# Weight words shifted in PSUM, 128-row tiles of v, and another order of the first chunk

## The chip, the cores and the metric

The kernel runs on one core of one Trainium2 chip. The metric is the device time of one execution in microseconds (us); lower is better. A core has TensorE (PE; its weight loads are PEld), VectorE (DVE), ScalarE (ACT), GpSimd (POOL) and SyncE (SP), each with its own queue that is worked off in order, and 16 DMA engines. SBUF is the working memory. PSUM is where TensorE writes; it has 8 banks of 512 fp32 words for each of 128 partitions, and GpSimd does not work on it.

## The reference

Attention in which each query sees the keys fewer than 16 positions away and 24 block summaries (the maximum of each block's 32 keys, the mean of its 32 values), and behind it two dense layers with an ELU between them. Batch 4, 8 heads, 768 positions, head size 64; the dense layers are 512 to 2048 to 512.

```python
k_sum = k.reshape(B, H, nb, block, D).max(axis=3)
v_sum = v.reshape(B, H, nb, block, D).mean(axis=3)
scores_l = scale * np.matmul(q, k.transpose(0, 1, 3, 2))
mask_l = np.abs(pos[:, None] - pos[None, :]) < window
scores_s = scale * np.einsum('bhsd,bhnd->bhsn', q, k_sum) + np.log(block)
scores_all = np.concatenate([np.where(mask_l, scores_l, -1e9), scores_s], axis=-1)
a = softmax(scores_all)
out = np.matmul(a, np.concatenate([v, v_sum], axis=2))
h = x @ w_in                      # x: out, as 3072 tokens of 512
g = np.where(h > 0, h, np.exp(np.minimum(h, 0)) - 1)
return g @ w_out
```

The two weights come as 64-bit floats; everything else is fp32.

## The kernel before, in words

**Chunks and folds.** The 3072 tokens are worked in six chunks of 512. For a chunk, the 2048 inner columns are 16 folds of 128: layer 1 makes `h` (PSUM, 128x512), then `E` (exponential, ACT, L601), `ts` (DVE, L605), `stt` (DVE, L608) make the ELU in `e`, `G` (ACT, L613) rounds it to `gh`, `gl` (POOL, L618) takes what is left, and layer 2 adds into four accumulators `o0` to `o3`. Each product is three matmul series, high by high, high by low and low by high, so a fold is 24 matmuls of 128x512.

**Weights.** There are 32 weight tiles, two for each fold (j = 0 to 31, in the order in which they are needed). Each is loaded as 64-bit words (`w`, a DMA on SP) and turned into a high and a low fp32 part by a five-step conversion: `X` (POOL, L135) puts the low bits of the mantissa into the lower word; `M` (ACT, L140) scales the upper word into `cv`; `S` is two DVE instructions, L144, which shifts `cv` by three and joins it with the lower word, and L146, which sets the sign from the upper word; `H` (ACT, L152) rounds `cv` to the high part; `L` (POOL, L155) makes the low part. `cv` has two buffers, so `M` of tile j waits until `L` of tile j - 2 is done. All 32 conversions lie in the first chunk.

**Attention.** Chunk 0 (positions 0 to 511 of batch 0) is done in the opening by four pairs of heads: block maxima `max`, local scores `sl`, block scores `ss`, masked row minima `low` (L166), exponentials `exp` (L174), reciprocals `z`, scaling `norm` (POOL, L183), transposes `tr` (L192), copies `ptc`, products with the values `val` (L349). The values lie as windows of 96 rows. The means of v are products of a small matrix with those windows (`sums`, L375), copied to `vsx` by `spr` (L380), and enter the result by their own matmuls (`add`, L356). Everything later is done in groups of two pairs of heads and 256 positions (`gsc`, `glow`, `ge`, `gz`, `gn`, `gtr`, `gpc`, `gval`, `gxh`, `gxl`: scores, minima, exponentials, reciprocals, scaling, transposes, copies, values, and the split of the result). A group's scores and transposes use the PSUM banks `a0` and `a1`. Groups 0 to 3 and the scores of group 4 belong to the first chunk. `mmul` (L482) makes the means of batch 1, in bank `a1`.

**Order.** The opening and the first chunk, up to fold 15's layer 1, are written out as a list of words, FIRST (L40), which sets the order on all five engines; each word is one of the functions above (`first.0` to `first.3` are fold 0's layer 1, `L1h` and `L1l` later layer 1, `L2a` to `L2c` layer 2). From fold 16 on a loop (L731) sets PE and SP, and the compiler places the rest.

Of the kernel before, what the change touches and what calls it, by code (L numbers as in the profile page):

```python
# [32 lines left out]
UW = 4  # L33
# [7 lines left out]
    max.0 sl.0 ss.0 low.0.0 max.1 exp.0.0 sl.1 low.0.1 ss.1 max.2 exp.0.1 low.1.0 sl.2 low.1.1 ss.2 idle.1  # L41
    exp.1.0 max.3 sl.3 exp.1.1 z.0.0 z.0.1 low.2.0 ss.3 idle.1 norm.0.1 low.2.1 norm.0.0 tr.0.1 z.1.0 exp.2.1
    sums.0 z.1.1 norm.1.0 low.3.0 tr.0.0 norm.1.1 low.3.1 exp.2.0 ptc.0.1.0 w.0 ptc.0.0.0 sums.1 exp.3.0 z.2.1
    tr.1.1 z.2.0 w.1 norm.2.0 tr.1.0 ptc.1.1.0 val.0 exp.3.1 z.3.0 q.0 ptc.1.0.0 norm.3.0 sums.2 z.3.1 tr.2.0
    norm.3.1 spr.0.0 spr.1.1 w.2 spr.2.1 val.1 spr.3.1 vm ptc.2.0.0 X.0 tr.3.0 norm.2.1 M.0 add.0 w.3 ptc.3.0.1
# [5 lines left out]
    X.8 M.7 G.2 S.7 L2c.1 H.6 gl.2 w.12 gval.0 H.7 L.6 sv.0 gsc.1 gxh.0 L.7 M.8 S.8 w.13 L1h.3 X.9 X.10 gxl.0
    H.8 w.14 M.9 L1l.3 L.8 glow.1.0 S.9 L2a.2 E.3 sv.1 K.2 X.11 M.10 L2b.2 X.12 ts.3 H.9 stt.3 L2c.2 L.9 S.10
    G.3 L1h.4 ge.1.0 gl.3 glow.1.1 H.10 L1l.4 gz.1.0 M.11 L.10 q.2 L2a.3 E.4 S.11 ge.1.1 gn.1.0 L2b.3 ts.4 w.15
    L2c.3 X.13 stt.4 H.11 gz.1.1 G.4 L1h.5 ks.0 M.12 gl.4 w.16 S.12 L.11 L1l.5 sv.2 ks.1 H.12 L2a.4 gn.1.1 M.13
    ks.3 L2b.4 E.5 w.17 L.12 ks.2 L2c.4 ts.5 pm.2 gtr.1.0 stt.5 w.18 X.14 L1h.6 gpc.1.0.1 S.13 G.5 sv.3 M.14
    gl.5 H.13 S.14 L1l.6 X.16 gtr.1.1 w.19 vs.1 L.13 L2a.5 gpc.1.1.1 H.14 L2b.5 E.6 X.15 w.20 ts.6 L.14 L2c.5
    M.15 stt.6 gval.1 G.6 vs.3 M.16 w.21 gl.6 S.15 gsc.2 gxh.1 X.17 gxl.1 L1h.7 H.15 w.22 L.15 S.16 L1l.7 X.18
    w.23 vs.0 H.16 L.16 L2a.6 E.7 vs.2 M.17 L2b.6 ts.7 w.24 K.3 X.19 M.18 stt.7 L2c.6 S.17 G.7 L1h.8 gl.7 S.18
    H.17 L.17 L1l.8 glow.2.0 H.18 L.18 mmul glow.2.1 E.8 q.3 L2a.7 ts.8 ge.2.1 X.20 stt.8 L2b.7 X.21 w.25 L2c.7
    G.8 gz.2.1 ge.2.0 L1h.9 gl.8 w.26 gn.2.1 M.19 gz.2.0 L1l.9 M.20 S.19 gn.2.0 mact mm w.27 L2a.8 E.9 S.20 H.19  # L60
# [5 lines left out]
    L1h.13 gz.3.1 M.28 gl.12 H.27 S.28 L1l.13 L.27 H.28 L2a.12 E.13 gn.3.1 L2b.12 ts.13 L.28 stt.13 L2c.12 G.13
    gl.13 gtr.3.0 L1h.14 gpc.3.0.1 X.29 X.30 M.29 L1l.14 X.31 S.29 M.30 gtr.3.1 E.14 L2a.13 ts.14 H.29 stt.14
    gpc.3.1.1 L.29 L2b.13 S.30 G.14 L2c.13 gl.14 M.31 gval.3 H.30 S.31 L.30 gsc.4 gxh.3 H.31 gxl.3 L1h.15 L.31
    glow.4.0 glow.4.1 ge.4.0 L1l.15 L2a.14 E.15 gz.4.0 ge.4.1 gn.4.0 ts.15 L2b.14 stt.15 L2c.14 G.15 gz.4.1
    gl.15 gn.4.1  # L70
# [4 lines left out]
def attn_elu_ffn(ctx: ExitStack, tc: tile.TileContext, qT, kT, vT, v, w_in, w_out, out):  # L75
# [139 lines left out]
    def first_units():  # L215
# [69 lines left out]
        nc.gpsimd.memset(pair, 1.0 / BLK)
        for sign, base in ((1, -E), (-1, E + BLK - 1)):
            nc.gpsimd.affine_select(out=pair, in_=pair, compare_op=ALU.is_ge, fill=0.0,
                                    base=base, pattern=[[-sign * BLK, 2]], channel_multiplier=sign)
        for p in range(NP):
# [6 lines left out]
        nc.sync.dma_start(out=v_t[0][E:KB, 0, :], in_=src[0:KB - E, :])  # L296
        for w0, w1 in ((1, UW), (UW, W2), (W2, W2 + 2), (W2 + 2, W2 + 3)):
            first_w = windows_of(w0)
            tile_ = v_t[w0 // UW] if w0 < W2 else v_own[(w0 - W2) // 2]
            at = w0 % UW if w0 < W2 else w0 % 2  # L300
            windows = bass.AP(tensor=src.tensor, offset=src.offset + (w0 * QW - E) * row,
                              ap=[[row, KB], [QW * row, w1 - w0], [1, row]])
            nc.sync.dma_start(out=tile_[0:KB, at:at + w1 - w0, :], in_=windows)
        nc.sync.dma_start(out=v_own[1][0:KB - E, 1, :], in_=src[S - KB + E:S, :])
# [9 lines left out]
        def scores(p, part):  # L314
# [4 lines left out]
            cols = slice(KB, KC) if part else slice(0, KB)  # L319
            for w in range(W2):  # L320
                for h in range(2):
                    rows, half = slice(h * D, (h + 1) * D), slice(w % 2 * QW, (w % 2 + 1) * QW)
                    right = ks[rows, p, :] if part else kn[p][rows, w * QW:w * QW + KB]
                    nc.tensor.matmul(banks_of[p, h][half, w // 2, cols], q_p[rows, w * QW:(w + 1) * QW], right,  # L324
                                     start=True, stop=True)
# [484 lines left out]
```

## Time and profile before

| | |
|---|---|
| median of 3 runs | 664.14 us (662.65 to 671.2) |
| the profiled execution | 664.48 us, of which the span of its instructions is 662.7 us |
| TensorE busy | 629.1 us (95%) |
| VectorE busy | 299.1 us (45%) |
| ScalarE busy | 273.4 us (41%) |
| GpSimd busy | 259.9 us (39%) |
| mean granted clock of TensorE | 0.984 |

The shares are means over stretches that differ: the opening, the first chunk with its 32 conversions, and 80 folds that only multiply. A stretch is therefore read by itself. The matmuls are pipelined, and one whose clock is halved counts as busy for twice as long.

### The profile page before, as it was taken

The page shows a single profiled execution, that of the slowest core. Times are in us where ns is not written, and L with a number is a line of the kernel's source. Part 1 is how long each engine was busy: PE and PEld are TensorE (multiplying, and loading weights), DVE is VectorE, ACT ScalarE, POOL GpSimd, SP SyncE. Part 2 cuts the span into 40 slices and gives each one's busy share as a digit, 9 for nine tenths or more (in the row PEclk, how much of TensorE's full clock was granted, in tenths as well). Part 3 has the DMA queues.
Part 4 walks back from the last instruction along what each step waited for, and adds up shares of the span by engine and source line. Part 5 has one row for each costly group of instructions (what it writes and reads, how often), then busy time and mean ns, then how long its engine had stood idle before and what let it go on. Part 6 is the DMA issues. An engine that isn't in the chain of part 4 may idle for free.

```text
span 662.7 us, 11510 instructions
## 1 busy us (share of the span) xinstructions
PE 629.1 (95%) x4368; PEld 505.9 (76%) x4368; DVE 299.1 (45%) x861; ACT 273.4 (41%) x745; POOL 259.9 (39%) x257
## 2 busy tenths in 40 slices
PE   7889795979999999999999999999999999999997
PEld 4667574857888888788888888888888888888885
DVE  7687998797332354232244343232432332322222
ACT  5565545565444244343343443343443443222222
POOL 4578776886332332322322332332332232222221
PEclk9899896999999999999999999999999999999999
DMA  9799082802120413521005313320320100100001
GB/s 270 218 383 295 34 253 72 254 1 61 66 61 1 133 50 108 164 66 32 29 25 154 104 48 87 102 65 10 115 63 9 30 1 1 64 0 1 0 1 63
DMA packets 63182, 57.95 MB, mean 87 GB/s; under 512 B 22616, under 2 KB 54872, under 8 KB 63128
## 3 DMA queue, kind: packets, MB, share of 16 engines
q1 hardware_dynamic: 59816, 51.33, 26.1%
q10 hardware_dynamic: 3312, 5.90, 2.3%
q8 instruction: 34, 0.56, 0.3%
q14 instruction: 20, 0.16, 0.1%
HBM read 50.14 MB, written 6.29 MB: 85 GB/s over the span
## 4 chain that ended last, share of the span: by engine, by line
PE 80%; DVE 11%; issue 3%; DMA 2%; ACT 2%; POOL 1%; SPq 0%; ACTq 0%; DVEq 0%
PE h L585 33%; PE o L638 33%; DVE cv L144 4%; DVE cv L146 3%; PE t_ps L192 3%; PE o_ps L549 3%; PE s L513 2%; PE o L628 2%; PE h L596 1%; DMA n<-in_kT_dram 1%; DVE e L605 1%; PE idle L256 1%; PE s L324 1%; DVE sm L166 1%; DMA out_dram<-ot 1%
## 5 line engine op out<-in xcount | busy, mean ns | idle before, releaser
L618 POOL TENSOR_TENSOR gl<-e,gh 128x512 fp32r<-128x512 f32 x96 | 126.9, 1322 | 286.7 <-ACT gh L613 210.2
L585 PE MATMUL h<-xh,w 128*128 128x512 f32 x640 | 214.2, 395 | 0.0
L638 PE MATMUL o<-w,gh 128*128 128x512 f32 x648 | 164.9, 392 | 0.5 <-DVE ot L659 0.5
L605 DVE TENSOR_SCALAR e<-e 128x512 f32<-128x512 f32 x96 | 46.3, 482 | 246.6 <-ACT e L601 245.0
L585 PEld LDWEIGHTS h<-xh,w 128*128 128x128 f32 x640 | 120.1, 188 | 27.2 <-issue 2.8
L638 PEld LDWEIGHTS o<-w,gh 128*128 128x128 f32 x648 | 120.2, 188 | 25.5 <-DVE ot L659 1.2
L601 ACT ACTIVATE e<-h 128x512 f32<-128x512 f32 x96 | 57.0, 594 | 167.4 <-PE h L585 161.7
L585 PE MATMUL h<-xl,w 128*128 128x512 f32 x320 | 124.5, 389 | 0.0
L613 ACT CAST gh<-e 128x512 fp32r<-128x512 f32 x96 | 59.6, 621 | 98.6 <-DVE e L608 98.5
L638 PE MATMUL o<-w,gl 128*128 128x512 f32 x324 | 89.4, 390 | 0.0
L183 POOL TENSOR_TENSOR sm<-sm,z 128x480 f32<-128x480 f32 x40 | 44.9, 1124 | 69.1 <-DVE z L180 50.2
L638 PEld LDWEIGHTS o<-w,gl 128*128 128x128 f32 x324 | 60.7, 188 | 13.1 <-POOL gl L618 0.5
L585 PEld LDWEIGHTS h<-xl,w 128*128 128x128 f32 x320 | 60.2, 188 | 11.4
L608 DVE SCALAR_TENSOR_TENSOR e<-h,e 128x512 f32<-128x512 f32 x96 | 66.4, 692 | 3.3
L174 ACT ACTIVATE sm<-sm,mx 128x120 f32<-128x120 f32 x160 | 60.9, 383 | 15.5 <-DVE mx L166 15.5
L155 POOL TENSOR_TENSOR w<-cv,w 128x512 fp32r<-128x512 f32 x32 | 44.2, 1388 | 21.8 <-ACT w L152 19.4
L596 PE MATMUL h<-xh,w 128*128 128x512 f32 x120 | 40.5, 399 | 1.8 <-ACT w L152 1.5
L628 PE MATMUL o<-w,gh 128*128 128x512 f32 x120 | 35.6, 421 | 6.7 <-ACT gh L613 6.7
L144 DVE SCALAR_TENSOR_TENSOR cv<-cv,raw_w 128x512 uint32<-128x512 uint32 x32 | 35.8, 1120 | 10.6 <-ACT cv L140 7.6
L146 DVE SCALAR_TENSOR_TENSOR cv<-raw_w,cv 128x512 uint32<-128x512 uint32 x32 | 36.7, 1147 | 1.1
L563 DVE TENSOR_TENSOR xl<-o_ps,xh 128x256 fp32r<-128x256 f32 x40 | 15.1, 417 | 45.8 <-ACT xh L556 45.8
L628 PEld LDWEIGHTS o<-w,gh 128*128 128x128 f32 x120 | 23.9, 205 | 13.7 <-ACT gh L613 8.4
(104 smaller groups left out, 584.8 us busy)
## 6 DMA issues: line engine op xcount, KB each, us to landing
raw_w<-in_w_in_dram SPq DMA_DIRECT2D x16, 512.0 KB
raw_w<-in_w_out_dram SPq DMA_DIRECT2D x16, 512.0 KB
qbd<-in_qT_dram SPq DMA_DIRECT2D x20, 256.0 KB
out_dram<-ot ACTq DMA_DIRECT2D x20, 256.0 KB
kw<-in_kT_dram SPq DMA_DIRECT2D x24, 144.0 KB
vw<-in_v_dram SPq DMA_DIRECT2D x24, 144.0 KB
n<-in_kT_dram SPq DMA_DIRECT2D x16, 192.0 KB
n<-in_vT_dram SPq DMA_DIRECT2D x16, 192.0 KB
```

Source lines behind the costliest of these rows:

```text
L144: nc.vector.scalar_tensor_tensor(out=bits, in0=bits, scalar=3, in1=self.lo, op0=ALU.logical_shift_left, op1=ALU.bitwise_or)
L146: nc.vector.scalar_tensor_tensor(out=bits, in0=self.hi, scalar=0x80000000, in1=bits, op0=ALU.bitwise_and, op1=ALU.bitwise_or)
L174: nc.scalar.activation(out=sm[:, t, :], in_=sm[:, t, :], func=AF.Exp, bias=mx[:, t, :], scale=-1.0, accum_out=z[:, t, :])
L585: nc.tensor.matmul(h_ps, w[:, a, cols], bb[:, cc, :], start=(k == 0), stop=(k == 3 * NCC - 1))
L596: nc.tensor.matmul(h_ps, w[:, lo, cc * P:(cc + 1) * P], bb[:, cc, :], start=(lo, cc, i) == (0, 0, 0), stop=(lo, cc) == (1, NCC - 1))
L601: nc.scalar.activation(out=e, in_=h_ps, func=AF.Exp)
L605: nc.vector.tensor_scalar(out=e, in0=e, scalar1=1.0, scalar2=-1.0, op0=ALU.min, op1=ALU.add)
L608: top = nc.vector.scalar_tensor_tensor(out=e, in0=h_ps, scalar=0.0, in1=e, op0=ALU.max, op1=ALU.add)
L613: nc.scalar.copy(out=gh, in_=e)
L618: nc.gpsimd.tensor_tensor(out=gl, in0=e, in1=gs[(c, f)][0].bitcast(F32), op=ALU.subtract)
L628: nc.tensor.matmul(o_acc[0][s], gs[(0, f)][a][:, s * P:(s + 1) * P], w[:, bb, :], start=(f, part) == (0, 0), stop=False)
L638: nc.tensor.matmul(o_acc[c][s], a[:, s * P:(s + 1) * P], w[:, bb, :], start=first and f == 0, stop=last and f == NF - 1)
```

## The change: what it does

**Weight words.** `M` writes its scaled word into a PSUM tile `sh` instead of `cv`. `sh` lies in bank `a0` for even j and in `a1` for odd j, the banks of the groups. L144 reads and writes `sh` there; the second instruction of `S` (now L147) reads the upper word from SBUF and `sh` from PSUM and writes `cv`, which is taken only then.

**Values.** In the opening, v lies as tiles of 128 rows (the windows of 96 rows begin at the same rows). `sums` uses six of them instead of twelve windows. The 24 rows behind each window's 96 are then overwritten by the block means with a DMA (`vm`), so that `val` takes local values and means in one matmul; the `add` matmuls are gone.

**Block scores.** `ss`, and the block scores of groups 0 and 1, are made for two query blocks at a time: 8 matmuls where there were 16.

**Order.** FIRST is another list: groups 0 to 2 begin two to three folds later and group 3 one, means and their copies lie ahead of the transposes, `idle` and `warm` add matmuls on zeros in the opening, and all five engines have another sequence. `mx` and `z` have 8 buffers instead of 4. The loop from fold 16 on is the same.

```diff
-    S.1 M.2 add.2 X.3 S.2 add.3 w.5 xh.2 H.1 xl.2 first.0 xh.3 L.1 H.2 xl.3 w.6 first.1 L.2 first.2 M.3 S.3 sk.1
+    S.2 L.1 M.3 first.1 w.6 first.2 xl.3 H.2 X.4 S.3 M.4 first.3 L.2 sk.1 L1h.1 E.0 ts.0 H.3 w.7 stt.0 L.3 M.5
...
         def exponent(self):
-            self.cv = ffn.tile([P, WC], F32, tag="cv", name="cv", bufs=2)
-            nc.scalar.mul(out=self.cv, in_=self.hi.bitcast(F32), mul=2.0 ** -112)
+            self.sh = psum.tile([P, WC], F32, tag=f"a{self.j % 2}", name="sh")
+            nc.scalar.mul(out=self.sh, in_=self.hi.bitcast(F32), mul=2.0 ** -112)
 
         def join(self):
-            bits = self.cv.bitcast(U32)
+            bits = self.sh.bitcast(U32)
             nc.vector.scalar_tensor_tensor(out=bits, in0=bits, scalar=3, in1=self.lo,
                                            op0=ALU.logical_shift_left, op1=ALU.bitwise_or)
-            nc.vector.scalar_tensor_tensor(out=bits, in0=self.hi, scalar=0x80000000, in1=bits,
+            self.cv = ffn.tile([P, WC], F32, tag="cv", name="cv", bufs=2)
+            nc.vector.scalar_tensor_tensor(out=self.cv.bitcast(U32), in0=self.hi, scalar=0x80000000, in1=bits,
                                            op0=ALU.bitwise_and, op1=ALU.bitwise_or)
...
+                    if part:
+                        nc.tensor.matmul(banks_of[p, h][:, w // 2, KB:KC], q_p[rows, w * QW:(w + 2) * QW], ks[rows, p, :],
+                                         start=True, stop=True)
...
-                                     windows_of(w)[0:KB, p * P + h * D:p * P + (h + 1) * D],
-                                     pts[p][0:KB, h, w // 2, w % 2 * QW:(w % 2 + 1) * QW],
-                                     start=w == 0, stop=False)
-
-        def add_means(p):
-            for h in range(2):
-                nc.tensor.matmul(o_of[p][h * D:(h + 1) * D].rearrange("p w q -> p (w q)"),
-                                 vsx[KB:KC, p, h * D:(h + 1) * D],
-                                 pts[p][KB:KC, h].rearrange("p t q -> p (t q)"), start=False, stop=True)
+                                     windows_of(w)[0:KC, p * P + h * D:p * P + (h + 1) * D],
+                                     pts[p][0:KC, h, w // 2, w % 2 * QW:(w % 2 + 1) * QW], start=True, stop=True)
...
+            "vm": lambda i: all_means(nc.sync, (*v_t, *v_own)[i], (UW, UW, 2, 2)[i]),
```

In the next rows, names ending in `HW` with a digit are DMA completions, and the engine names in brackets are what an instruction waits for. First the sync queue in the opening, before: two weight tiles, queries, a third weight tile, then the means for group 0's windows.

```order
L116 DMA raw_w1_0_439<-in_w_in_dram 128x4x128 [waits DMAHW6_49]
L116 DMA raw_w1_1_472<-in_w_in_dram 128x4x128 [waits DMAHW7_49]
L416 DMA qbd0_70<-in_qT_dram 128x2x256 [waits DMAHW0_49]
L116 DMA raw_w2_0_534<-in_w_out_dram 128x512 [waits DMAHW1_49]
L384 DMA v_own_104<-vsx_103 24x2x512 [waits DMAHW2_49,DVE_49,Activation_49]
L384 DMA v_own_105<-vsx_103 24x2x512 [waits DMAHW3_49]
L116 DMA raw_w1_2_569<-in_w_in_dram 128x4x128 [waits DMAHW4_49]
L116 DMA raw_w2_1_585<-in_w_out_dram 128x512 [waits DMAHW5_49]
```

The same place in the changed kernel, from the last tile of v on.

```order
L313 DMA vxl_107<-in_v_dram 128x4x512 [waits DMAHW5_49]
L116 DMA raw_w1_0_386<-in_w_in_dram 128x4x128 [waits DMAHW6_49]
L116 DMA raw_w1_1_412<-in_w_in_dram 128x4x128 [waits DMAHW7_49]
L393 DMA vxh_106<-vsx_103 24x4x512 [waits DMAHW2_49,DMAHW0_49,DVE_49]
L393 DMA vxl_107<-vsx_103 24x4x512 [waits DMAHW5_49,DMAHW1_49]
L426 DMA qbd0_70<-in_qT_dram 128x2x256
L116 DMA raw_w2_0_476<-in_w_out_dram 128x512 [waits DMAHW3_49]
L116 DMA raw_w1_2_508<-in_w_in_dram 128x4x128 [waits DMAHW4_49]
L316 DMA v_own_104<-in_v_dram 128x512
L317 DMA v_own_105<-in_v_dram 80x512 [waits DMAHW6_49]
L393 DMA v_own_104<-vsx_103 24x2x512 [waits DMAHW7_49,DMAHW5_49,PE_49]
L393 DMA v_own_105<-vsx_103 24x2x512 [waits DMAHW0_49,PE_49]
```

Two DMAs of means, for the opening's own values, now stand behind the second weight tile, and two for the windows of the groups behind the fourth; the third weight tile is behind the first pair.

VectorE at the conversions of tiles 9 and 10 (fold 5's layer 1 and fold 4's layer 2), before.

```order
L144 SCALAR_TENSOR_TENSOR cv<-cv,raw_w_5_798 128x512 [waits DMAHW6_49,Activation_49,Pool_49]
L146 SCALAR_TENSOR_TENSOR cv<-raw_w_5_798,cv 128x512 [waits DVE_49]
L605 TENSOR_SCALAR e<-e 128x512 [waits Activation_49]
L608 SCALAR_TENSOR_TENSOR e<-h,e 128x512 [waits DVE_49]
L144 SCALAR_TENSOR_TENSOR cv<-cv,raw_w_4_830 128x512 [waits DMAHW7_49,Activation_49]
L146 SCALAR_TENSOR_TENSOR cv<-raw_w_4_830,cv 128x512 [waits DVE_49]
```

VectorE at the same two tiles in the changed kernel.

```order
L144 SCALAR_TENSOR_TENSOR sh<-sh,raw_w_5_714 128x512 [waits DMAHW2_49,Activation_49,Pool_49]
L147 SCALAR_TENSOR_TENSOR cv<-raw_w_5_714,sh 128x512 [waits DVE_49,Pool_49]
L144 SCALAR_TENSOR_TENSOR sh<-sh,raw_w_4_736 128x512 [waits DMAHW3_49,Activation_49,Pool_49]
L147 SCALAR_TENSOR_TENSOR cv<-raw_w_4_736,sh 128x512 [waits DVE_49,Pool_49]
L615 TENSOR_SCALAR e<-e 128x512 [waits Activation_49]
L618 SCALAR_TENSOR_TENSOR e<-h,e 128x512 [waits DVE_49]
```

The second instruction of `S` now waits for GpSimd (the `L` of two tiles before), a wait that stood on ScalarE's `M`; the two pairs follow each other, where the ELU of fold 3 stood between them.

TensorE at the means of batch 1 (`vsps`), before: between fold 8's layer 1 and fold 7's layer 2.

```order
L596 MATMUL h<-xh,w_8_1278 128x512 [waits Pool_49]
L596 MATMUL h<-xh,w_8_1278 128x512 x3
L482 MATMUL vsps<-ident,vst 32x128 [waits DVE_49,PE_49]
L482 MATMUL vsps<-ident,vst 32x128 x3
L628 MATMUL o_779<-w_7_1293,gh 128x512 [waits Activation_49]
L628 MATMUL o_780<-w_7_1293,gh 128x512
```

The same products in the changed kernel.

```order
L638 MATMUL o_688<-w_8_1295,gh 128x512
L638 MATMUL o_689<-w_8_1295,gh 128x512
L492 MATMUL vsps<-ident,vst 32x128 [waits DVE_49,PE_49]
L492 MATMUL vsps<-ident,vst 32x128 x3
L606 MATMUL h<-xh,w_10_1340 128x512 [waits DVE_49,Activation_49]
L606 MATMUL h<-xl,w_10_1340 128x512
```

They moved three half folds down: behind fold 7's layer 2, fold 9's layer 1 and fold 8's layer 2, in front of fold 10's layer 1.

## Rows read from the trace of the kernel before

**Rows 1.** Busy time of each engine in three stretches of the span.

```profile
core 0: us, PE busy (x) PEld busy (x) DVE busy (x) ACT busy (x) POOL busy (x), PEclk, DMA share, GB/s
0.00:35.51 35.51, 29.08 (x537) 19.45 (x537) 25.40 (x114) 20.24 (x79) 16.81 (x48) 0.95 0.85 253
35.51:166.94 131.43, 109.41 (x766) 84.48 (x765) 113.76 (x209) 73.28 (x181) 101.65 (x88) 0.94 0.51 164
166.94:662.70 495.76, 490.65 (x3069) 401.93 (x3067) 159.92 (x540) 179.90 (x488) 141.47 (x122) 1.00 0.19 55
```

**Rows 2.** TensorE in order of time, the opening and the first loop row.

```profile
22.69 0.57 PE L349 MATMUL o_ps<-pt_own,vxh 96*64 96x64 f32 x13 [2.28 <-issue]
33.64 1.93 PE L356 MATMUL o_ps<-pt_own,vsx 24*64 24x512 f32 x8
35.51 0.50 PE L397 MATMUL h<-xh,w 128*128 128x512 f32 x1
...
166.94 0.39 PE L585 MATMUL h<-xh,w 128*128 128x512 f32 x1
```

**Rows 3.** What TensorE waited for, 35.51 to 166.94 us.

```profile
PE vsps L482 <- DVE mx L166: 7.6, 1, 7.6
PE o L628 <- ACT gh L613: 6.7, 4, 2.2
PE o L628 <- POOL gl L618: 3.6, 7, 1.3
PE h L596 <- ACT w L152: 1.5, 1, 1.5
```

**Rows 4.** The chain that ended last, 60 to 84 us, shares by line.

```profile
by line: DVE cv L146 28.0%; DVE cv L144 26.2%; DVE ks L475 10.8%; issue 8.9%; ACT cv L140 8.4%; DVE e L605 8.2%; POOL w L155 5.4%; DVE sm L166 3.2%; DVE e L608 3.1%; DVE xl L563 1.4%; ACT w L152 0.3%; DVE mx L166 0.1%; ACTq L152 0.1%; ACT g
```

**Rows 5.** One of three stretches at the lower clock, as in Rows 1.

```profile
108.40:113.30 4.90, 4.90 (x17) 3.88 (x14) 3.33 (x8) 3.79 (x14) 4.37 (x6) 0.55 0.01 3
```

**Rows 6.** Groups of instructions up to 167 us, different shapes apart.

```profile
L146 DVE SCALAR_TENSOR_TENSOR cv<-raw_w,cv 128x512 uint32<-128x512 uint32 x32 | 36.7, 1147 | 1.1
L144 DVE SCALAR_TENSOR_TENSOR cv<-cv,raw_w 128x512 uint32<-128x512 uint32 x32 | 35.8, 1120 | 10.6 <-ACT cv L140 7.6 <-POOL raw_w L135 2.8
L608 DVE SCALAR_TENSOR_TENSOR e<-h,e 128x512 f32<-128x512 f32 x15 | 10.4, 691 | 0.5
L155 POOL TENSOR_TENSOR w<-cv,w 128x512 fp32r<-128x512 f32 x32 | 44.2, 1388 | 21.8 <-ACT w L152 19.4 <-ACT xh L361 1.9 <-PE h L596 0.3
L135 POOL TENSOR_SCALAR raw_w<-raw_w 128x512 uint32<-128x512 uint8 x32 | 27.7, 867 | 2.7
L356 PE MATMUL o_ps<-pt_own,vsx 24*64 24x512 f32 x16 | 4.1, 606 | 0.0
```

**Rows 7.** Single lines of code: duration in ns, shortest, median and longest.

```profile
L144 DVE SCALAR_TENSOR_TENSOR cv<-cv,raw_w x32: 677/1138/1798, 27.3 to 162.3; 128x512 uint32<-128x512 uint32 x32
L608 DVE SCALAR_TENSOR_TENSOR e<-h,e x15: 690/692/692, 41.4 to 158.8; 128x512 f32<-128x512 f32 x15
L155 POOL TENSOR_TENSOR w<-cv,w x32: 1267/1297/1742, 31.3 to 164.8; 128x512 fp32r<-128x512 f32 x32
L135 POOL TENSOR_SCALAR raw_w<-raw_w x32: 653/974/1149, 23.7 to 157.5; 128x512 uint32<-128x512 uint8 x32
```

**Rows 8.** VectorE in order of time, 43 to 57 us.

```profile
43.59 1.77 DVE L144 SCALAR_TENSOR_TENSOR cv<-cv,raw_w 128x512 uint32<-128x512 uint32 x1
56.45 0.68 DVE L144 SCALAR_TENSOR_TENSOR cv<-cv,raw_w 128x512 uint32<-128x512 uint32 x1
```

**Rows 9.** What ScalarE and VectorE waited for, 35.51 to 166.94 us.

```profile
ACT cv L140 <- POOL w L155: 6.4, 7, 1.7
DVE cv L144 <- ACT cv L140: 7.4, 5, 3.1
```

**Rows 10.** A DMA issue of the sync queue, in order of time.

```profile
26.51 1.82 SPq L384 DMA_DIRECT2D v_own<-vsx  x2
```

**Rows 11.** DMA traffic from 9 to 18 us: all that moved.

```profile
DMA packets 1146, 2.20 MB, mean 245 GB/s; under 512 B 80, under 2 KB 80, under 8 KB 1144
```

More of the change, by code (lines that the diff above doesn't have):

```diff
@@ L40 @@
 FIRST = """
[L41 to L45, printed above, removed]
@@ L51 @@
[L51 to L55, printed above, removed]
@@ L56 @@
[L56 to L60, printed above, removed]
@@ L66 @@
[L66 to L70, printed above, removed]
+    ve vo max.0 sl.0 max.1 ss.0 sl.1 low.0.1 low.0.0 ss.1 exp.0.1 idle.1 max.2 sl.2 exp.0.0 low.1.1 ss.2 idle.1
@@ L129, in __init__ @@
         def __init__(self, j):
-            self.key = order[j]
+            self.j, self.key = j, order[j]
             self.raw = raws.pop(self.key)
@@ L171, in exps @@
         if z is None:
-            z = att.tile([P, UW, 1], F32, tag="z", name="z", bufs=4)
+            z = att.tile([P, UW, 1], F32, tag="z", name="z", bufs=8)
         for t in range(UW):
@@ L279, in first_units @@
         make_identity(nc, ident)
-        pair = mean[:, BLK:BLK + 2]
+        blocks = mean[:, BLK - 1:BLK + 4]
         nc.gpsimd.memset(mean, 0.0)
[L285 to L289, printed above, removed]
+        nc.gpsimd.memset(blocks, 1.0 / BLK)
+        for sign, base in ((1, E), (-1, E - 1)):
+            nc.gpsimd.affine_select(out=blocks, in_=blocks, compare_op=ALU.is_ge, fill=0.0,
+                                    base=base, pattern=[[-sign * BLK, 5]], channel_multiplier=sign)
+        nc.gpsimd.tensor_copy(out=mean[:, 2 * BLK:3 * BLK], in_=mean[:, BLK:2 * BLK])
+        nc.gpsimd.memset(mean[0:E, 2 * BLK + NS - 1:2 * BLK + NS], 1.0 / BLK)
+        for p in reversed(range(NP)):
             nc.gpsimd.memset(kw[p][:, UW - 1, KB - E:KB], 0.0)
@@ L295, in first_units, with rows, load_even, load_odd @@
         src = v[0]
[L296 to L304, printed above, removed]
+        def rows(first, n):
+            return bass.AP(tensor=src.tensor, offset=src.offset + first * row, ap=[[row, P], [P * row, n], [1, row]])
+        def load_even():
+            nc.sync.dma_start(out=v_t[0][E:P, 0, :], in_=src[0:P - E, :])
+            nc.sync.dma_start(out=v_t[0][0:E, 0, :], in_=src[S - E:S, :])
+            nc.sync.dma_start(out=v_t[0][:, 1:UW, :], in_=rows(P - E, UW - 1))
+            for i in range(2):
+                nc.sync.dma_start(out=v_own[i][:, 0:1, :], in_=rows((UW + i) * P - E, 1))
+        def load_odd():
+            nc.sync.dma_start(out=v_t[1], in_=rows(QW - E, UW))
+        def load_last():
+            nc.sync.dma_start(out=v_own[0][:, 1:2, :], in_=rows(UW * P + QW - E, 1))
+            nc.sync.dma_start(out=v_own[1][0:KB - E, 1, :], in_=src[S - KB + E:S, :])
         def maxima(p):
@@ L318, in scores @@
                     banks_of[p, h] = psum.tile([P, UW, KC], F32, tag=tags[p][h], name="s")
-            cols = slice(KB, KC) if part else slice(0, KB)
-            for w in range(W2):
+            for w in range(0, W2, 2) if part else range(W2):
                 for h in range(2):
[L322 to L325, printed above, removed]
+                    rows = slice(h * D, (h + 1) * D)
+                    if part:
+                        nc.tensor.matmul(banks_of[p, h][:, w // 2, KB:KC], q_p[rows, w * QW:(w + 2) * QW], ks[rows, p, :],
+                                         start=True, stop=True)
+                    else:
+                        half = slice(w % 2 * QW, (w % 2 + 1) * QW)
+                        nc.tensor.matmul(banks_of[p, h][half, w // 2, 0:KB], q_p[rows, w * QW:(w + 1) * QW],
+                                         kn[p][rows, w * QW:w * QW + KB], start=True, stop=True)
         def low(p, h):
@@ L404, in first_units @@
             "z": recip, "norm": norm, "tr": trans, "ptc": lambda p, h, i: take_t(p, h, copies[i]), "val": vals,
-            "add": add_means, "xh": take_h, "xl": take_l, "sums": lambda i: sums(parts[i]), "first": first,
-            "spr": lambda p, i: spread(p, copies[i]), "idle": idle,
-            "vm": lambda: [all_means(nc.sync, tile_, 2) for tile_ in v_own],
+            "xh": take_h, "xl": take_l, "sums": lambda i: sums(parts[i]), "first": first,
+            "spr": lambda p, i: spread(p, copies[i]), "idle": idle, "warm": lambda n: idle(n, tag="o3"),
+            "ve": load_even, "vo": load_odd, "vl": load_last,
+            "vm": lambda i: all_means(nc.sync, (*v_t, *v_own)[i], (UW, UW, 2, 2)[i]),
         }
```

94 lines of the change are left out of this document (57 added, 37 removed).

## The prediction

> **What bounds the kernel now.** I read the span in three stretches first [rows 1]: the opening up to the first matmul of fold 0 at 35.51 us, the first chunk up to the loop's first matmul at 166.94 us [rows 2], and the loop. In the loop TensorE is busy 490.65 of 495.76 us at the full clock; the change leaves the loop's order as it is, so those 495.8 us stay. In the first chunk (131.43 us) no engine is full: VectorE 113.8, TensorE 109.4, GpSimd 101.7, ScalarE 73.3 us. Then I read what TensorE waits for there [rows 3]: it idles 131.43 - 109.41 = 22.0 us, of which four entries make 19.4. The largest, 7.6 us, ends with VectorE's row minima, which must be out of bank `a1` before the means of batch 1 can enter it; the next, 6.7 us, ends with ScalarE's `gh`, which itself follows VectorE's ELU. The chain of waits says who is late: from 60 to 84 us the two instructions of `S` alone are 54% of it [rows 4]. So VectorE bounds the first chunk. [...] The work of TensorE in the first chunk is therefore 109.4 - 5.4 = 104.0 us, and 27.4 us of the 131.4 are idle time or lost clock.
>
> Why VectorE is so full: `S` takes 1.120 + 1.147 us for each of 32 tiles [rows 6]. The same instruction takes from 677 to 1798 ns [rows 7], 1.77 us in one place and 0.68 in another [rows 8]. An ELU instruction of the same size, `stt` at L608, which takes one input from PSUM and one from SBUF, takes 690 to 692 ns in all 15 cases, on the same engine, in the same stretch, beside the same GpSimd work [rows 7]. GpSimd's own instructions vary too, `L` from 1267 ns with a mean of 1388, `X` from 653 with a mean of 867 [rows 6, 7]. I read this as two engines that hold each other up when a VectorE instruction takes both inputs from SBUF.
>
> **The change part by part.**
>
> *`S` with one input in PSUM.* Both its instructions become like L608. 32 x (1.120 + 1.147 - 2 x 0.691) = 28.3 us less on VectorE, which leaves 113.8 - 28.3 = 85.5 us. No row shows VectorE writing PSUM. The bounds are nothing gained, if the write costs what the contention cost, and 32 x (2.267 - 0.677 x 2) = 29.2 us, by the shortest L144; I take 28.3, since L608 is the nearest row. [...]
>
> *GpSimd.* Without that contention `L` can fall by 1388 - 1267 ns and `X` by 867 - 653 ns, 32 x 0.335 = 10.7 us [rows 6, 7], to 91 us; at worst it stays at 101.7. `ts` still meets it, so I count half, 96 us, and nothing of it in the time, because TensorE has more to do.
>
> *`M` into PSUM.* No row shows ScalarE writing PSUM from SBUF. ScalarE is busy 73 of 131 us; up to 0.2 us more or less for each of 32 is 6 us either way beside TensorE's 104, and costs nothing.
>
> *The wait that moves.* `M` waited for `L` of two tiles before, 6.4 us in seven waits, and `S` for `M`, 7.4 us in five [rows 9]. Now the second half of `S` waits for that `L`, with the ELU of the current fold queued behind it on VectorE. In return a tile's round from `L` to the next `L` on its buffer is half of `S`, `H` and `L` instead of all five steps. At best 7.4 us of VectorE's waiting goes, at worst 6.4 us come to it; VectorE has 131.4 - 85.5 us to spare, so I take nothing.
>
> *Banks.* The conversions now share `a0` and `a1` with five score sets and eight transposes of the first chunk: at 13 places TensorE waits for an `S`, and `M` waits for the minima or the copy of the transposes. The order puts `S` half a fold or so ahead of most of these. One finished late costs between nothing and a whole `S`, 2 x 0.69 = 1.4 us; most often it will be there, and I take 0.25 us, 13 x 0.25 = 3.2 us.
>
> *The opening.* On TensorE the `add` matmuls go: 16 passes, 4.1 us [rows 6], the last of them the 1.93 us directly ahead of fold 0 [rows 2]; with them may go the 2.28 us in which it waited at 22.69 us [rows 2], for nothing that the profile shows. Half of the mean products go as well. What comes is a wait: `val.0` now needs the means written into v by two DMAs of 192 KB, which stand behind two weight tiles on the sync queue. The copies `spr` can be done right after the minima, some 8 us before the 26.51 us at which the sync queue now issues its means [rows 10], so at about 18 to 19 us. But 6.3 MB move ahead of them (keys and queries 2.6, v 2.6, two weight tiles 1.05 MB): 25 us at the opening's mean of 253 GB/s [rows 1], which has an empty stretch in it, some 22 without that; and the two DMAs, 0.4 MB, need 1.6 us at the 245 GB/s at which v has moved [rows 11]. I put `val.0` at 24 us; from there four `val` and the transposes, about 6 us, to fold 0 at 30 to 31 us instead of 35.51. So 5 us gained; if the DMAs land 5 us later, nothing, and if the order holds without a stall, 8. On the sync queue everything behind the means gains: it stood still until 26.51 us, and the third weight tile is now issued some 7 us sooner.
>
> *With one answer.* Block scores by two query blocks take half of 1.2 us of groups 0 and 1, 0.6 us off TensorE; in the opening they lie beside VectorE. Groups that begin later bring the same work to another place. More buffers of `mx` and `z`, the memsets and the added zero matmuls lie beside other work.
>
> *The sum.* Work of TensorE 104.0 - 0.6 = 103.4 us. Of the 22.0 us of waits, those that end with VectorE or with what it had just handed on (7.6, 6.7, 1.5) go, 15.8 us, and so does the lost clock that followed them. What is left is 22.0 - 15.8 = 6.2, and 3.2 for the banks: 103.4 + 9.4 = 112.8 us, 18.6 less than 131.4. With 5 us of the opening the gain is 23.6, against the profiled execution's 664.48 us: 640.9, so 641 us. That execution is 0.3 us above the median of the runs, which changes nothing. TensorE is then the fullest engine, 103 of 113 us, and GpSimd the next late one.
>
> **The rivals.**
>
> *GpSimd takes VectorE's place.* It has 101.7 us now and at the least 91, in a queue that mixes `X`, `L`, `gl` and the scaling of the groups. For it: 3.6 us of TensorE's waits end with `gl` already [rows 3], and `S` now waits for `L`. Against it: its longest waits now are for others. If it stays at 101.7 and fills the chunk as VectorE does now (113.8 of 131.4, 87%), the chunk takes 117.4 us: 664.5 - 14.0 - 5 = 645.5, and 650 with waits on top.
>
> *The change does not free VectorE.* If the spread of `S` comes from the words 8 bytes apart or from the write and not from the second SBUF input, VectorE keeps its 113.8 us, the chunk loses only what the order gives, at most the 7.6 us wait, and the time is 664.5 - 5 - 4 = 655 (650 to 662). Against it: the 677 ns cases read the same words.
>
> *The banks tie TensorE to the conversions.* At 13 places scores or transposes must wait for an `S`, which waits for an `L`, and no `M` can start until a group's minima are read. At 23.6 / 13 = 1.8 us more for each place the gain is gone; at 3 us each, a whole `S`, an `M` and an `H` behind a busy queue, 13 x 3 = 39 us stand against the 26.8 that the rest gives (23.6 + 3.2): 664.5 + 12 = 677, more if the clock falls as it did after the 7.6 us wait. For it: `a1` is where the largest wait is now. Against it: VectorE and ScalarE have more than a quarter of the stretch free.
>
> **How the numbers follow.** The forecast has 0.63, GpSimd's bound 0.22, a VectorE that is not freed 0.10, the banks 0.05. The range: its low end is the chunk with 2 us of waits and 8 us from the opening, 664.5 - 26 - 8 = 631; its high end lets 18 us of waits stand and the opening give 2, 664.5 - 10 - 2, so about 653, and 655 takes in half of the case in which VectorE is not freed. What is left out is the banks and the rest of that case. A measurement of this kernel can tell about 2% from no change, that is below 651 us. Of the forecast 95% is below it, of GpSimd's case 85%, of the next 10%: 0.80 faster. Same: 0.16. Slower: 0.04.
>
> **What would show it.** In the changed kernel both halves of `S` at 0.68 to 0.72 us with hardly any spread; `L` near 1.27 us; VectorE near 85 us in the first chunk; the loop's first matmul near 143 us and fold 0 near 30; the 7.6 us wait gone and no stretch of lower clock in the chunk; the loop again 495.8 us long. Wrong would be: `S` still above 1 us (the second rival); TensorE's waits ending with GpSimd for more than 10 us (the first); waits of scores and transposes for L147 above 1 us each (the third); or `val.0` after 28 us, waiting for a DMA.

## Result and the profile after

The changed kernel takes 642.3 us (median of 4 runs, 640.44 to 643.07) and the kernel before 667.0 in the runs beside it (median of 4, 662.65 to 671.2): a ratio of 0.963, 95% interval 0.955 to 0.970. It is faster, and the forecast of 641 us is 1.3 us off. The four runs before lie in two pairs, 662.65 and 664.14 us and 669.92 and 671.2; the profiled execution, 664.48, from which the forecast was worked out, belongs to the lower pair, and against it the gain is 22.3 us where 23.6 were forecast.

The profiled execution took 642.2 us with a span of 640.1. First the busy times in the three stretches that answer to [rows 1], with fold 0 at 31.13 us and the loop's first matmul at 144.13 us, and then one stretch at the lower clock, which answers to [rows 5]:

```profile
core 0: us, PE busy (x) PEld busy (x) DVE busy (x) ACT busy (x) POOL busy (x), PEclk, DMA share, GB/s
0.00:31.13 31.13, 30.00 (x426) 20.29 (x426) 23.87 (x115) 18.64 (x76) 15.46 (x49) 1.00 0.82 273
31.13:144.13 113.00, 104.65 (x737) 84.29 (x734) 88.25 (x214) 73.17 (x187) 90.97 (x91) 0.97 0.63 205
144.13:640.10 495.97, 490.45 (x3069) 402.15 (x3067) 158.68 (x537) 178.62 (x480) 139.68 (x121) 1.00 0.19 55
42.28:47.43 5.15, 5.15 (x13) 4.09 (x14) 4.60 (x6) 3.27 (x6) 4.67 (x4) 0.55 1.06 389
```

The loop is what it was (495.97 against 495.76 us). The opening is 4.4 us shorter, the first chunk 18.4. VectorE's busy time in the chunk fell from 113.76 to 88.25 us, GpSimd's from 101.65 to 90.97; TensorE, 104.65 of 113.00 us, is now by far the fullest engine. The lines of `S`, `L` and `X` (shortest, median and longest in ns; `S` is L144 and L147 now, `L` L156, `X` L135) answer to [rows 7]:

```profile
L144 DVE SCALAR_TENSOR_TENSOR sh<-sh,raw_w x32: 689/693/700, 28.3 to 135.6; 128x512 uint32<-128x512 uint32 x32
L147 DVE SCALAR_TENSOR_TENSOR cv<-raw_w,sh x32: 686/689/690, 29.1 to 136.4; 128x512 uint32<-128x512 uint32 x32
L156 POOL TENSOR_TENSOR w<-cv,w x32: 1266/1295/1467, 30.6 to 137.9; 128x512 fp32r<-128x512 f32 x32
L135 POOL TENSOR_SCALAR raw_w<-raw_w x32: 642/658/718, 25.5 to 132.6; 128x512 uint32<-128x512 uint8 x32
```

The 677 to 1798 ns of the first half of `S` have become 689 to 700. What TensorE waits for in the chunk (us in total, times, longest) answers to [rows 3]:

```profile
PE o L638 <- ACT gh L623: 4.7, 1, 4.7
PE t_ps L193 <- DVE cv L147: 1.8, 1, 1.8
PE s L516 <- DVE cv L147: 1.5, 2, 1.0
PE h L406 <- DVE xl L374: 0.3, 1, 0.3
```

The 7.6 us for the row minima are gone, and no wait ends with GpSimd. But one of 4.7 us for `gh` stands there, at 42.28 us, and behind it fold 0's twelve layer-2 matmuls take 5.15 us at a mean granted clock of 0.55 (0.50 until 46.90 us, 1.00 after that); the twelve of fold 1 take 2.72. The chain of waits before it (start, us, what) goes back to a transfer:

```profile
34.38 6.67 DMA raw_w<-in_w_in_dram
41.07 0.25 ACT sh L140
41.63 0.61 ACT gh L623
42.28 5.15 PE o L638 x12
```

ScalarE stood 2.6 us at `M.5` (`sh` L140), waiting for its weight tile, with `G.0` (`gh`) queued behind it; `M.4` ahead of it had waited 2.4 us for its own. Why were the tiles late? SyncE's queue in order of time (start, us of issue), and what SyncE waited for at L393 from 20 to 40 us:

```profile
25.12 0.43 SPq L317 DMA_DIRECT2D v_own<-in_v_dram  x1
31.11 1.72 SPq L393 DMA_DIRECT2D v_own<-vsx  x2
32.88 0.51 SPq L116 DMA_DIRECT2D raw_w<-in_w_out_dram  x1
34.38 0.47 SPq L116 DMA_DIRECT2D raw_w<-in_w_in_dram  x1
```

```profile
SPq L393 <- DMA v_own<-in_v_dram: 5.5, 1, 5.5
```

Between the issue at 25.12 and the one at 31.11 us SyncE issued nothing: it stood 5.5 us at the two DMAs of the block means into the last two v tiles (`vm.2`, `vm.3`, L393), which wait for the rows of v that had just been asked for. Weight tile 4 (32.88) and tile 5 (34.38) stand behind them.

### The profile page after: what moved, and what is told of

It is laid out like the page before. It is cut to its first block, busy times and chain, and to the rows that moved or that the text cites. A ratio compares the mean times of both kernels' runs of the same rounds, so it can differ in the third digit from the quotient of the medians.

```text
span 640.1 us, 11234 instructions
## 1 busy us (share of the span) xinstructions
PE 625.1 (98%) x4226; PEld 506.7 (79%) x4226; DVE 270.8 (42%) x864; ACT 270.4 (42%) x742; POOL 246.1 (38%) x259
## 4 chain that ended last, share of the span: by engine, by line
PE 90%; DVE 4%; DMA 2%; ACT 2%; issue 1%; SPq 0%; DVEq 0%; ACTq 0%
PE h L595 34%; PE o L648 34%; PE o L638 5%; PE h L606 4%; PE t_ps L193 3%; PE o_ps L559 3%; PE s L516 3%; PE idle L258 2%; DVE sh L144 1%; DMA raw_w<-in_w_in_dram 1%; DVE cv L147 1%; PE o_ps L365 1%; DVE e L615 1%; DMA out_dram<-ot 1%; PE s L336 1%
## 5 line engine op out<-in xcount | busy, mean ns | idle before, releaser
L628 POOL TENSOR_TENSOR gl<-e,gh 128x512 fp32r<-128x512 f32 x96 | 123.8, 1290 | 283.2 <-ACT gh L623 216.4
L156 POOL TENSOR_TENSOR w<-cv,w 128x512 fp32r<-128x512 f32 x32 | 41.9, 1315 | 6.1 <-ACT w L153 5.1
L167 DVE CUSTOM_DVE_ANT_0 sm<-s,mask 128x120 f32<-128x120 f32 x160 | 33.9, 277 | 3.4 <-PE s L523 2.2
L175 ACT ACTIVATION_READ_ACCUMULATOR sm<-sm,mx 128x1 f32 x160 | 30.1, 188 | 0.0
```

The lines of the kernel that those rows point to most:

```text
L156: nc.gpsimd.tensor_tensor(out=self.w[:, 1, :], in0=self.cv, in1=self.w[:, 0, :].bitcast(F32), op=ALU.subtract)
L628: nc.gpsimd.tensor_tensor(out=gl, in0=e, in1=gs[(c, f)][0].bitcast(F32), op=ALU.subtract)
```

## Experiments

**1. The word back in SBUF.** In the changed kernel (part of the edit):

```
-            self.sh = psum.tile([P, WC], F32, tag=f"a{self.j % 2}", name="sh")
-            nc.scalar.mul(out=self.sh, in_=self.hi.bitcast(F32), mul=2.0 ** -112)
+            self.cv = ffn.tile([P, WC], F32, tag="cv", name="cv", bufs=2)
+            nc.scalar.mul(out=self.cv, in_=self.hi.bitcast(F32), mul=2.0 ** -112)
```

and both halves of `S` on `cv`; `M.2`, `M.4`, `M.6`, `M.7`, `M.13`, `M.17`, `M.23`, `M.29` stand behind `L.0`, `L.2` and so on in `FIRST`.

> The changed kernel with its PSUM part alone undone: ScalarE writes the word into cv in SBUF and both halves of S work there; where the changed order would now let M.j wait for a buffer that L.(j-2) has yet to free (eight places), M.j stands right behind L.(j-2). Opening, block scores and the rest of the order stay. Theory (S is stretched because it reads two SBUF operands beside GpSimd): the halves of S go back from 0.69 us to means of about 1.1 us with a spread from 0.68 to 1.8, X from 0.66 towards 0.9, VectorE's busy time in the first chunk from 88 to about 115 us, and the time to 655 to 665 us. Rival (it is the new order and the earlier opening that shortened the chunk, the place of the word adds little): the halves of S stay under 0.85 us and the time within 3 us of 642.

Measured: 660.6 us (659.95 to 663.26, 10 runs), 0.9935 of before (0.990 to 0.997). The chunk and the loop, columns as above, and the groups of the chunk (count, then busy us and mean ns, then idle time ahead):

```profile
30.90:159.40 128.50, 111.79 (x736) 85.59 (x733) 118.08 (x208) 72.71 (x178) 104.37 (x89) 0.95 0.56 180
159.40:659.40 500.00, 492.69 (x3069) 403.10 (x3067) 161.16 (x544) 180.89 (x491) 141.69 (x122) 0.99 0.19 55
```

```profile
L143 DVE SCALAR_TENSOR_TENSOR cv<-cv,raw_w 128x512 uint32<-128x512 uint32 x32 | 31.8, 994 | 4.5 <-ACT cv L139 3.6 <-POOL raw_w L134 0.9
L145 DVE SCALAR_TENSOR_TENSOR cv<-raw_w,cv 128x512 uint32<-128x512 uint32 x32 | 41.4, 1293 | 1.1
L134 POOL TENSOR_SCALAR raw_w<-raw_w 128x512 uint32<-128x512 uint8 x32 | 27.3, 852 | 3.3 <-DMA raw_w<-in_w_out_dram 0.8
L154 POOL TENSOR_TENSOR w<-cv,w 128x512 fp32r<-128x512 f32 x32 | 46.8, 1463 | 16.0 <-ACT w L151 15.6
```

The theory holds: `S` is back at 0.99 and 1.29 us, VectorE at 118 us, and with the changed order kept the chunk takes 128.5 us against 131.4 before. The last conversions spill into the loop, which begins with waits of 1.9 us and 3.4 us at a granted clock of 0.50 and takes 500 us. So the order and the opening alone are worth 3.5 us by the medians of these runs (664.14 and 660.6), with the eight `M` standing elsewhere than in the changed order.

**2. The PSUM part alone, in the kernel before.** `exponent` and `join` as in the change; the word takes `a0` or `a1`, and in before's `FIRST` nine words move ahead where two users of a bank would cross (`glow.0.0` ahead of `M.4`, `S.16` ahead of `gsc.2`, `mact` ahead of `M.19`, and six like the first).

> The kernel before with the PSUM part alone: the word of each tile lies in bank a0 or a1. Its order is kept, apart from nine words that the shared banks force ahead (group maxima ahead of M.4, M.8, M.9, M.17, M.18, M.24 and M.25, S.16 ahead of a group's scores, the means' copy ahead of M.19). The opening stays as before (first fold at 35.5 us). Theory: S at 0.69 us with hardly any spread, VectorE's busy time in the chunk down by about 28 us, the chunk from 131 to 112 to 120 us, and the time 645 to 653 us: some three quarters of the whole gain. Rival (order): S may be 0.69 us, but the waits move to the forced places and the time stays above 657 us.

Measured: 651.9 us (647.05 to 656.25), 0.979 of before (0.970 to 0.988). The three stretches of the profiled execution, 648.61 us:

```profile
0.00:33.70 33.70, 28.45 (x537) 18.37 (x537) 25.27 (x115) 20.10 (x79) 16.50 (x48) 0.95 0.86 257
33.70:149.80 116.10, 105.61 (x766) 83.63 (x765) 85.93 (x211) 73.90 (x188) 88.12 (x88) 0.97 0.58 188
149.80:646.60 496.80, 490.76 (x3069) 402.06 (x3068) 158.50 (x537) 178.25 (x480) 140.31 (x121) 1.00 0.19 55
```

The chunk falls from 131.43 to 116.10 us with VectorE at 85.93. The PSUM part alone gives 2.1% of the time, the rest alone (experiment 1) 0.65%, both together 3.7%. The 1% or so that is left over lies within these intervals, so that the two together give more than each by itself is not shown; that in experiment 1 4.2 us are lost again in the loop would fit it. The opening, in which only the first conversions differ from before's, ended at 33.70 us here and at 35.51 in before's profile. There the 2.28 us of waiting [rows 2] were followed by 3.4 us at a granted clock of 0.50 (24.0 to 27.4 us). Here the wait was 0.75 us; the lower clock lies earlier, with means of 0.84 from 9 to 18 us and 0.96 from 18 to 26, and from 26 us to the end of the opening it is 1.00. So up to 1.8 of the 4.4 us by which the changed opening is shorter may hang on where one execution meets such a stretch; the changed opening has none.

**3. One half of `S` with two SBUF operands.** In the changed kernel the first half writes `cv`, and the second works on `cv`:

```
-            bits = self.sh.bitcast(U32)
-            nc.vector.scalar_tensor_tensor(out=bits, in0=bits, scalar=3, in1=self.lo, ...)
+            self.cv = ffn.tile([P, WC], F32, tag="cv", name="cv", bufs=2)
+            bits = self.cv.bitcast(U32)
+            nc.vector.scalar_tensor_tensor(out=bits, in0=self.sh.bitcast(U32), scalar=3, in1=self.lo, ...)
```

> The changed kernel with the place of the word undone for one half of S only: the first half reads the bank and writes cv, the second half reads and writes cv, so that it alone has two SBUF operands. Order, opening and banks stay. Theory (each half is stretched by itself, when both of its operands lie in SBUF beside a busy GpSimd): the first half stays at 0.69 us with no spread, the second goes to 1.0 to 1.25 us with a spread up to 1.8; VectorE's busy time in the first chunk rises by 10 to 18 us to some 98 to 106, the time to 644 to 652 us. Rival (the stretch comes from writing SBUF, or from any of the two being late): both halves rise, or neither.

Measured: 644.0 us in one run. The two halves (shortest, median, longest) and the chunk:

```profile
L145 DVE SCALAR_TENSOR_TENSOR cv<-sh,raw_w x32: 673/690/693, 28.7 to 139.6; 128x512 uint32<-128x512 uint32 x32
L147 DVE SCALAR_TENSOR_TENSOR cv<-raw_w,cv x32: 691/896/1427, 29.5 to 140.3; 128x512 uint32<-128x512 uint32 x32
31.50:146.80 115.30, 106.75 (x736) 83.69 (x733) 98.14 (x212) 73.57 (x187) 99.58 (x90) 0.99 0.63 201
```

Only the half with two SBUF operands spreads; the other, reading the same words 8 bytes apart and now writing SBUF, stays at 0.69. So neither the strided words nor the write does it. The size was at the edge: 1.00 to 1.25 us were expected, the mean is 0.93. The one run is 1.7 us above the changed kernel's median: VectorE, at 98 us, and GpSimd, at 100, are still below TensorE's 107. In experiment 1 VectorE, at 118 us, has passed TensorE, at 112, and the time is 660.6 us.

**4. GpSimd relieved, `S` in SBUF.** The kernel of experiment 1, but it leaves out the subtraction that makes a weight's low part; ScalarE writes a copy of `cv` in its place:

```
-            nc.gpsimd.tensor_tensor(out=self.w[:, 1, :], in0=self.cv, in1=self.w[:, 0, :].bitcast(F32), op=ALU.subtract)
+            nc.scalar.copy(out=self.w[:, 1, :], in_=self.cv)
```

> The kernel of the first experiment (word in SBUF) with GpSimd relieved of L: the low part of each weight is written by ScalarE as a plain copy of cv, so the subtraction is left out and the low parts are wrong; GpSimd keeps X, gl and the scaling of the scores. Its busy time in the chunk falls from 104 to some 55 us, ScalarE's rises by about 20. Theory (the halves of S are stretched only while GpSimd works on SBUF at the same time): the means of the halves fall from 0.98 and 1.26 us to 0.75 to 0.95, with many at 0.68 and some up to 1.8, X falls from 0.85 towards 0.66 to 0.8, and the time falls below 652 us though S still reads two SBUF operands. Rival (two SBUF operands cost this by themselves, or it is ScalarE's traffic that stretches them): the means stay above 1.05 us, or rise.

Measured: 646.2 us in one run. The chunk, and then VectorE and GpSimd in order of time near 63 us (start, us):

```profile
31.40:147.50 116.10, 106.07 (x736) 83.68 (x733) 95.07 (x210) 87.75 (x214) 57.48 (x58) 0.97 0.62 200
```

```profile
62.00 0.69 DVE L143 SCALAR_TENSOR_TENSOR cv<-cv,raw_w 128x512 uint32<-128x512 uint32 x1
62.72 0.69 DVE L145 SCALAR_TENSOR_TENSOR cv<-raw_w,cv 128x512 uint32<-128x512 uint32 x1
63.33 1.78 DVE L143 SCALAR_TENSOR_TENSOR cv<-cv,raw_w 128x512 uint32<-128x512 uint32 x1
...
62.73 1.83 POOL L625 TENSOR_TENSOR gl<-e,gh 128x512 fp32r<-128x512 f32 x1 [1.35 <-issue]
64.53 1.43 POOL L181 TENSOR_TENSOR sm<-sm,z 128x480 f32<-128x480 f32 x1
```

`S` fell to means of 0.83 and 0.97 us (the second a little over what was expected), with more traffic on ScalarE, so ScalarE's traffic is not what stretches it. `X` did not fall: its mean is 0.84 us, against 0.85 in experiment 1. The rows show how the two engines meet. `gl` began at 62.73, just behind a half of `S`, and is 1.83 us long instead of 1.29. The next `S` (63.33) lasts until 65.11, 0.55 us after `gl` ends at 64.56; and the scaling that begins at 64.53 takes 1.43 us instead of the 0.99 that it takes undisturbed. Here they take turns by whole instructions. Counted by start and end over the whole chunk, 25 of the 64 halves here overlap by less than 0.1 us with a GpSimd instruction, and all 25 take 0.68 to 0.70 us; in before it is 12 of 64, again 0.68 to 0.70, while the other 52 have a mean of 1.24. In the changed kernel 55 of 64 overlap, and they take 0.69 all the same. So, of the halves with two SBUF operands, none takes more than 0.70 us without such an overlap, and with it one takes up to 1.78 us here and 1.80 us in before.

**5. The means of the last two v tiles later.** In `FIRST` of the changed kernel:

```
-    ... xh.0 vl vm.2 vm.3 val.1 ... w.8 X.5 ...
+    ... xh.0 vl val.1 ... w.8 vm.2 vm.3 X.5 ...
```

> The changed kernel with one move on SyncE's queue: the two DMAs that write the block means into the last two v tiles (vm.2, vm.3) are issued behind weight tile 8 instead of ahead of weight tile 4. Theory: in the changed kernel SyncE stands from 25.1 to 31.1 us at these two, so weight tiles 4 and 5 land only at 37 and 41 us, ScalarE's M.4 and M.5 wait 2.4 and 2.6 us for them with G.0 queued behind, and TensorE waits 4.7 us for gh and then works 2.4 us longer at the lower clock. With the move the weights are issued by 26 us, that wait falls under 1 us, the slow stretch goes, and the time is 634 to 637 us. Rival (the transfers are bound by their bytes, or M.4 and M.5 find the next late thing): the wait stays above 3 us and the time within 1.5 us of 642.

Measured: 637.05 us (636.27 to 637.79), 0.957 of before (0.951 to 0.963), 5.3 us below the changed kernel's median and just at the end of the 634 to 637 us expected. SyncE's queue, the chunk, and TensorE's largest waits:

```profile
24.90 0.43 SPq L317 DMA_DIRECT2D v_own<-in_v_dram  x1
25.37 0.42 SPq L116 DMA_DIRECT2D raw_w<-in_w_out_dram  x1
27.05 0.61 SPq L116 DMA_DIRECT2D raw_w<-in_w_in_dram  x1
33.86 1.71 SPq L393 DMA_DIRECT2D v_own<-vsx  x2
```

```profile
30.90:138.60 107.70, 102.82 (x734) 82.59 (x733) 86.30 (x214) 73.42 (x187) 90.88 (x91) 1.00 0.67 211
```

```profile
PE s L516 <- DVE cv L147: 2.5, 2, 1.7
PE o L638 <- ACT gh L623: 0.9, 1, 0.9
```

Weight tile 4 is issued at 25.37 us instead of 32.88, tile 5 at 27.05 instead of 34.38. The wait for `gh` is 0.9 us instead of 4.7, the clock of the chunk 1.00 instead of 0.97. `gval.0`, which needs these means, loses nothing.

**6. Block scores by one query block again.** In the opening and in groups 0 and 1:

```
-                for t in range(0, UW, 2):
+                for t in range(UW):
...
-                        nc.tensor.matmul(s_of[g, h][:, 2 * i + t // 2, KB:KC], q_t[rows, i, t * QW:(t + 2) * QW], ...
+                        nc.tensor.matmul(s_of[g, h][half, 2 * i + t // 2, KB:KC], q_t[rows, i, t * QW:(t + 1) * QW], ...
```

> The changed kernel with the block scores, of the opening and of the first two groups, again by one query block of 64 columns (32 matmuls a pair instead of 16). Theory (a matmul of 24 columns costs by its weight columns: 128 columns take 64 ns or so, 64 columns 19 ns): each group's block scores fall from 1.07 to about 0.61 us, each of the opening's four from 1.07 to 0.66 us; TensorE's work in the chunk falls by 0.9 us, the time by up to 1 us. Rival (the 1.07 us is where the instruction stands, at the head of a wait or beside other matmuls, not its shape): the 32 take 1.07 us or more, and the time rises by half a microsecond or nothing.

Measured: 640.5 us in one run, within the spread of the changed kernel's. Its rows are clear, first the changed kernel's group 0, then this one's:

```profile
53.65 1.07 PE L523 MATMUL s<-ks,qbd 64*128 64x24 f32 x16
```

```profile
54.02 0.61 PE L522 MATMUL s<-ks,qbd 64*64 64x24 f32 x32
```

32 matmuls with 64 weight columns take 0.61 us, 16 with 128 columns 1.07. TensorE's busy time is lower by 1.7 us than the changed kernel's 30.00 in the opening and by 0.7 than its 104.65 in the chunk.

**7. Both edits.** Experiments 5 and 6 together.

> The changed kernel with the two single edits that came out ahead of it: the means of the last two v tiles issued behind weight tile 8 (alone 637.05 us), and block scores by one query block (alone 640.5 us in one run, TensorE's work 1.7 us less in the opening and 0.7 us less in the chunk). Theory: the chunk's 0.7 to 0.9 us come on top, since TensorE bounds the chunk now (102.8 of 107.7 us busy); the opening's 1.7 us don't, since its end did not move with them: 635.5 to 636.7 us. Rival: the waits for banks grow by what the matmuls save: 637 us.

Measured: 633.65 us (633.15 to 635.75, 6 runs), 0.951 of before (0.945 to 0.958), the best kernel here; its slowest run is 4.7 us below the fastest of the changed kernel. The chunk:

```profile
29.90:135.20 105.30, 101.76 (x768) 81.47 (x765) 84.72 (x214) 73.51 (x187) 91.15 (x91) 1.00 0.69 217
```

The gain beyond experiment 5 is 3.4 us, more than expected. In the chunk TensorE works some 1 us less (101.76 against 102.82) and waits 1.3 us less in all (3.5 against 4.9): 1.7 less for the banks of the scores (0.8 against 2.5), a little more elsewhere. The opening ended at 29.9 us, against 30.9 in experiment 5, but at 31.0 in the next kernel, which has the same opening; as far as one execution of each tells, that 1 us is no effect of the edit.

**8. Scores behind the next layer-1 part.** The kernel of experiment 7 with, in `FIRST`, `gsc.0` behind `L1h.3`, `gsc.1` behind `L1h.6`, `gsc.2` behind `L1h.9`.

> The previous kernel with the scores of groups 0, 1 and 2 each moved behind the next fold's first layer-1 part on TensorE, since with the means issued later TensorE waits 2.5 us at the second and third of them, and at their issue, for a half of S that still holds the bank. Theory: those waits (2.5 us, and up to 2.8 us of issue time around them) go, the softmax of these groups has slack, and the time is 632 to 635 us. Rival: the softmax is late for the transposes and values behind it, VectorE and ScalarE stand at the maxima, and the time is 636 us or more.

Measured: 637.6 us (635.86 to 638.7), 4 us worse than experiment 7: the rival. In the profiled executions 3.1 us of it lie in the chunk (108.5 us against 105.5) and 1.1 in the opening, which the move doesn't touch. TensorE's waits, and VectorE near 50 to 60 us:

```profile
PE t_ps L193 <- DVE cv L147: 3.3, 1, 3.3
PE h L605 <- DVE e L617: 1.9, 2, 1.2
```

```profile
50.65 0.28 DVE L167 CUSTOM_DVE_ANT_0 sm<-s,mask 128x120 f32<-128x120 f32 x1 [1.36 <-PE s L522]
54.25 0.69 DVE L147 SCALAR_TENSOR_TENSOR cv<-raw_w,sh 128x512 uint32<-128x512 uint32 x1
59.62 0.69 DVE L147 SCALAR_TENSOR_TENSOR cv<-raw_w,sh 128x512 uint32<-128x512 uint32 x1
```

The scores' waits for banks are gone, but VectorE stood 1.36 us for the scores at 50.65, the conversions and the ELU queued behind the minima came later, and the transposes of group 0 then waited 3.3 us for a half of `S` that held their bank. Layer 1 waited 1.9 us for the ELU, too. Without the move TensorE waited 0.8 us at the scores and 0.9 at these transposes.

## Why the prediction was right, step by step

**`S` with one PSUM operand**, 28.3 us: right, and with it the second rival fell. 32 x (2.267 - 0.694 - 0.688) = 28.3 us on `S` itself; VectorE fell by 25.5, with 214 instructions in the stretch where 209 were. That `S` is stretched where it has two SBUF operands beside a busy GpSimd is shown by experiments 1, 3 and 4: means of 0.99 and 1.29 us, of 0.93 for the one such half, and of 0.83 and 0.97 beside less GpSimd work. The operand in PSUM has no price that these runs show: 694 and 688 ns on average, against 0.68 to 0.70 us for the undisturbed halves with two SBUF operands.

**GpSimd**, 96 us, 91 at least: it took 90.97, and no wait of TensorE ends with it. The first rival, GpSimd as the bound, fell: the contention that slowed `S` had slowed GpSimd as well, and both got the time back.

**Banks**, 13 x 0.25 = 3.2 us: 3.3 us (1.8 and 1.5). That the sums agree is luck, for the waits stand at 3 places and not at 13, and one of them, 1.8 us, is above the 1 us that the prediction gave as a sign of its third rival; the price of that rival, 39 us, is far off. **The moved wait**, nothing: `S` waits for no `L`, and 7.6 us for `M`, as before (7.4). **The opening**, 5 us: 4.4, `val.0` at 25.14 us (24 said). No run separates its parts, and one was not in the prediction: before's opening had those 3.4 us at a granted clock of 0.50, some 1.7 us of work lost (half of 3.4).

**The lost clock**, 5.4 us: the sum takes it off TensorE's 109.4. No run shows that figure as such. What before's trace shows is three stretches of work at a lower clock, behind waits of TensorE of 1.96, 7.58 and 1.28 us that ended at 77.54, 107.83 and 147.23 us; [rows 5] is the second, and these are the first and the third (columns as in [rows 1]):

```profile
78.92:82.29 3.37, 3.37 (x8) 2.61 (x9) 3.34 (x4) 1.11 (x2) 3.37 (x3) 0.54 0.00 0
147.23:150.70 3.47, 3.47 (x10) 2.73 (x11) 3.08 (x3) 0.24 (x1) 2.58 (x2) 0.56 0.00 0
```

That is 3.37 x 0.46 + 4.90 x 0.45 + 3.47 x 0.44 = 5.3 us.

**The waits that go**, 15.8 us, and with them the lost clock: here the step failed. The step said that the waits that end with VectorE, or with what it had just handed on, vanish. The 7.6 us did (they are gone in experiment 1 as well, so the new order alone removes them), but a wait for `gh` of 4.7 us remained, with a new cause, and 5.15 - 2.72 = 2.4 us of lost clock behind it. The prediction counted everything behind the means on SyncE's queue as gaining, because the third weight tile is issued sooner. It had not asked what `vm.2` and `vm.3` wait for, and that weight tiles 4 and 5 are queued behind them. Experiment 5 shows 5.3 us there. **Block scores**, -0.6 us: wrong in sign, +0.9 us in groups 0 and 1 (2 x (1.07 - 0.61)); the step halved the time with the count and left out the weight columns.

That the chunk still came out, 113.0 us against 112.8, is a balance of misses: 8.3 us of TensorE's waits are left where 9.4 were allowed (none with GpSimd, where 3.6 were), the lost clock adds 2.4, and TensorE's work without it is 104.65 - 2.4 = 102.2 where 103.4 was said, though block scores cost more. The rest of its work came out 2.7 us lower than before's rows made it. Most of that lies in layer 2: outside the stretches of lower clock, 25 of before's 154 matmuls there hold TensorE for 0.31 to 0.40 us, many of them the last ahead of a wait or the first behind one, where the others take 0.22 to 0.25; in the changed kernel it is 10 of 169, which makes some 2.3 us. So a wait that goes can take more with it than its idle time, which is all that the prediction had counted.
